# Attention into sorted rows: per-side waits for the copies of batch 7, and fewer comparisons of counts

## The chip, the cores and the metric

The kernel runs on 1 core of a Trainium2 chip. The metric is the device time of one execution in microseconds (us). Three runs of the kernel before gave 193.85, 194.16 and 194.34 us; the median is 194.16 us.

## What is computed

The first half is an attention without a softmax over pairs: with 8 batches, 8 heads, 576 tokens and 64 channels per head, q is normalised by its exponentials over the channels, k by its exponentials over the tokens, kv = kᵀv per head, and the result is q·kv. The second half is a mixture of experts on the 4608 tokens with 512 channels:

```python
x = attn_out.transpose(0, 2, 1, 3).reshape(N, D)          # N = 4608, D = 512
logits = x @ w_gate + modality_bias[modality_id]
e_idx = argmax(logits, 1)
out[mask] = gate_w[mask, None] * (relu(x[mask] @ w1[e]) @ w2[e])   # for each expert e
```

The kernel takes it that each of the two modalities ends at the expert that its bias prefers. It therefore runs two experts only, counts at the end whether that was true, and has a loop over all experts for the case that it was not (it runs zero times on this data).

## The kernel before, in words

**Sorted rows.** The tile xs (128 partitions x 4 x 4608 columns, bf16) holds the attention's output transposed, one column per token, sorted by modality: side a fills from column 0 upwards, side b from column 4607 downwards. A batch has 9 groups of 64 tokens. Inside a group a permutation (line 1128) has brought the tokens of side a to the front. After the multiplication with kv (line 1167) the group lies in PSUM, and the function put (line 1183 and on) copies its 64 columns twice into xs (line 1198): once for side a at the number of a-tokens so far, once for side b. The place is a register value. Each copy writes all 64 columns, and what does not belong to its side is overwritten by a later copy of the same side. The very last group is written by both sides at the same place.

**What makes the copies wait.** As the place is not known ahead, the function window gives the framework a stand-in range of columns, and the framework makes a copy wait for earlier instructions that wrote or read the same stand-in range. In batches 0 to 6 the two sides have ranges of their own. In batch 7 both sides have the same one, the 64 columns around the middle column MID = 2304, so that each copy waits for the end of the copy before it, whichever side that was.

**Who copies.** A planner (class Plan, with a table of due times, TUNED) orders all work by a model of costs before anything is issued; its order is the order of each engine's queue. In batches 6 and 7 all 18 copies are on ScalarE (ACT). In batch 6 they alternate a, b, a, b. In batch 7 the order is b0 a0 b1 a1 b2, a ReLU (line 1274), then b3 a2 b4 a3 b5 a4 a5, then a load of two register values (line 1444) and a copy of a quarter of the expert weights (line 1467), then b6 a6 b7 a7 a8 b8.

**What reads the rows.** The function ffn runs a pass over 256 columns of one side: logits (line 1240), then the first matrix in four steps of 8 matmuls, function h_mm (line 1312), ReLU on VectorE (line 1276) or ScalarE (line 1274), the second matrix (line 1325), the scaling by the gate (line 1282) and an indirect DMA of the rows to DRAM (line 1285). Passes 0 to 6 of a side follow their batches. The four passes of batch 7 (two of each side, around MID) and one more for the tile in which the two sides meet wait for every copy of batch 7. PSUM has a ring of buffers; a buffer that a copy still reads can't be written by the next matmul.

**Around it on VectorE.** At the same time VectorE runs mid_run (lines 827 to 838), twelve small instructions that sort out the rows of the tile in the middle, the ReLUs and the evictions of line 1142. The code behind the plan (lines 1594 to 1644) checks counts: 16 comparisons of the running number of a-tokens (in aoff_x, one row) with limits (lines 1630 and 1633), a matmul that sums the tokens with the expected expert (line 1621), a minimum over all results (line 1641), and the number of times that the fallback loop runs. The framework places these instructions on its own, and the trace shows 15 of the comparisons between and right behind the instructions of mid_run.

Of the kernel before, what the change touches and what calls it, by code (L numbers as in the profile page):

```python
# [10 lines left out]
FP32 = mybir.dt.float32  # L11
# [4 lines left out]
ALU = mybir.AluOpType  # L16
# [3 lines left out]
P = 128  # L20
# [10 lines left out]
def view(t, dims, off=0, parts=None):  # L31
    p0 = t.ap[0]
    if parts is None:
        return bass.AP(tensor=t.tensor, offset=t.offset + off, ap=[list(p0)] + [list(d) for d in dims])
    lo, n = parts
    return bass.AP(
        tensor=t.tensor, offset=t.offset + lo * p0[0] + off, ap=[[p0[0], n]] + [list(d) for d in dims]
    )
# [206 lines left out]
def kernel(  # L245
# [12 lines left out]
    nc = tc.nc  # L258
    B, H, S, Dh = q.shape
    D = H * Dh  # L260
    N = B * S
# [3 lines left out]
    NJ = S // 64  # L265
    NC = B * NJ
# [4 lines left out]
    MID = N // 2  # L271
    TM = MID // P
    GW = 256
    RW = P

    passes_a = [(n, 256 * n, 256) for n in range(B)] + [(B - 1, 256 * B, 256)]
# [8 lines left out]
    def sb(shape, dtype, name):  # L285
        return pool.tile(shape, dtype, name=name)
# [43 lines left out]
    place = sb([P, NSL], FP32, "place")  # L330
# [316 lines left out]
    aoff_x = sb([1, NC + 1], FP32, "aoff_x")  # L647
# [9 lines left out]
    both = sb([P, 2, 2], FP32, "both")  # L657
# [203 lines left out]
    o_bsel = pl.op({"POOL": (2.3, 2.4, True)}, bsel_run, [o_aoff, o_exp], key="bsel", rank=13)  # L861
    o_mid = pl.op({"DVE": (1.0, 1.15, True)}, mid_run, [o_idx, o_bsel], key="mid", rank=74)

    def window(at, of_pass, T):

        n, lo, w = of_pass
        off = lo + (w - T) // 2 if n < B - 1 else MID - T // 2
        return bass.AP(
            tensor=xs.tensor,
            offset=xs.offset + at,  # L870
            ap=[list(xs.ap[0]), [N, KD], [1, T]],
            dep_tracking_offset=xs.offset + off,
        )

    final, edge, scaled_q = [], {}, []

    def sync(later, first, reason):
        tc.add_manual_dep(
            later.ins,
            first.ins.name,  # L880
            mybir.DependencyInfo(mybir.DependencyClass.Sync, mybir.DependencyReason.DATA),
            reason=reason,
        )
# [8 lines left out]
    def attention(b):  # L892
# [227 lines left out]
        for gi, (j0, nj) in enumerate(groups):  # L1120
            sbuf = Buf(r_ps)
            w = nj * 64
# [39 lines left out]
        for gi, (j0, nj) in enumerate(groups):  # L1162
            xbuf = Buf(r_ps)

            def s2(_, j0=j0, nj=nj, xbuf=xbuf):
                for c in range(KD):
                    nc.tensor.matmul(  # L1167
                        out=view(ps_t[xbuf.idx], [[1, nj * 64]], c * nj * 64),
                        lhsT=kvbd[kvb.idx][:, c, :],
                        rhs=et[etb.idx][:, c, j0 * 64 : (j0 + nj) * 64],  # L1170
                        start=True,
                        stop=True,
                    )

            o3 = pl.op(
                on_pe(*[nj * 64] * KD),
                s2,
                [ets[gi], o_kb],
                key=own_key(f"s2_{b}", j0), rank=R + 4,
                takes=[xbuf],  # L1180
                uses=[kvb, etb],
                lag=lag,
            )
            for jj in range(nj):
                for side in range(2):

                    def put(e, jj=jj, j0=j0, nj=nj, side=side, xbuf=xbuf):
                        c = b * NJ + j0 + jj
                        a = av[e][(j0 + jj) // 2]
                        if j0 + jj < NJ - 1:  # L1190
                            a = a >> 16 if jj else a & 0xFFFF
                        a = nc.s_assert_within(a, 0, 64 * c, skip_runtime_bounds_check_because=WHY)
                        if side:
                            a = a + (N - 64 - 64 * c)
                        p = next(x for x in (passes_b if side else passes_a) if x[0] >= b)
                        dst = window(a, p, 64)
                        src = view(ps_t[xbuf.idx], [[nj * 64, KD], [1, 64]], jj * 64)
                        w_ = nc.scalar.copy(out=dst, in_=src) if e == "ACT" else nc.vector.tensor_copy(out=dst, in_=src)  # L1198
                        if b >= 3 and not started["ab"[side]]:
                            started["ab"[side]] = True  # L1200
                            for before in id_ins:
                                sync(w_, before, "windows overlap the digits of places")
                        if not j0 + jj and b:
                            sync(w_, edge[side], "windows of the batch before reach into this one's")
                        if j0 + jj == NJ - 1:
                            edge[side] = w_
                        if b == B - 1:
                            final.append(w_)

                    before = win[-2] if len(win) > 1 else filled[b - 1][side - 2] if b else None  # L1210

                    across = win[-1 - 2 * side] if j0 + jj == NJ - 1 and b == B - 1 else None
                    same = before and before.costs.keys() == {copier[b][side]}
                    win.append(
                        pl.op(
                            on_dve(256) if copier[b][side] == "DVE" else on_act(256),
                            put,
                            [o3, o_id if b >= 3 else None, *los, None if same else before, across],
                            key=own_key(f"put{b}{side}", j0 + jj), rank=R + 4, gap=0.13,
                            uses=[xbuf],  # L1220
                        )
                    )
                    if same:
                        pl.follow(win[-1], before)
            if copier[b][0] != copier[b][1]:

                for o in win[-2 * nj + 1 :: 2]:
                    pl.later(o, win[-2])
# [8 lines left out]
    def logits(t0, nt, t, whole=False):  # L1237
        for i in range(nt):
            for c in range(KD):
                m = nc.tensor.matmul(  # L1240
                    out=t[:, i * E : (i + 1) * E],
                    lhsT=xs[:, c, (t0 + i) * P : (t0 + i + 1) * P],
                    rhs=wg_sb[:, c, :],
                    start=(c == 0),
                    stop=(c == KD - 1),
                )
                if whole and not i and not c:
                    for w_ in final[-2:]:
                        sync(m, w_, "every batch is in its places")

    def gates1(t0, nt, t):
# [50 lines left out]
    def h_mm(t, lo, w, slot_, f0, whole=False, kds=(0, KD)):  # L1302

        if kds == (0, KD // 2):

            nc.tensor.matmul(
                out=t[:, 0 : 2 * w], lhsT=zero, rhs=view(ones, [[0, 2 * w // P], [1, P]], 0, (0, 1)), start=True, stop=False
            )
        for i in range(2):
            for kd in range(*kds):  # L1310
                f = f0 + i
                m = nc.tensor.matmul(  # L1312
                    out=t[:, i * w : (i + 1) * w],
                    lhsT=w1(W[:, slot_, :], kd, f),
                    rhs=xs[:, kd, lo : lo + w],
                    start=(kd == 0 and kds == (0, KD)),
                    stop=(kd == KD - 1 and (i == 1 or kds == (0, KD))),
                )
                if whole and not f and not kd:
                    for w_ in final[-2:]:  # L1320
                        sync(m, w_, "every batch is in its places")

    def y_mm(t, h, i, slot_, c0=0, cn=D, kfs=(0, KF)):
# [283 lines left out]
    def keys():  # L1607
# [11 lines left out]
    nc.vector.tensor_copy(out=cnt_b, in_=cnt)  # L1619
    n_ps = ps_t[0]  # L1620
    nc.tensor.matmul(out=n_ps[:, 0:1], lhsT=ones, rhs=cnt_b, start=True, stop=True)
    early = sorted({(n, lo + w) for n, lo, w in passes_a if n < B - 1}) + [(B - 1, MID - RW)]
    ok = sb([1, 1 + 2 * len(early)], FP32, "ok")
    nc.vector.tensor_scalar(
        out=ok[:, 0:1], in0=n_ps[0:1, 0:1], scalar1=float(N) - 0.5, scalar2=None, op0=ALU.is_ge
    )
    for i, (n, need) in enumerate(early):
        so_far = aoff_x[0:1, NJ * (n + 1) : NJ * (n + 1) + 1]
        o_ = 1 + 2 * i
        nc.vector.tensor_scalar(  # L1630
            out=ok[:, o_ : o_ + 1], in0=so_far, scalar1=float(need), scalar2=None, op0=ALU.is_ge
        )
        nc.vector.tensor_scalar(
            out=ok[:, o_ + 1 : o_ + 2],
            in0=so_far,
            scalar1=float(S * (n + 1) - need),
            scalar2=None,
            op0=ALU.is_le,
        )
    okm = sb([1, 1], FP32, "okm")  # L1640
    nc.vector.tensor_reduce(out=okm, in_=ok, op=ALU.min, axis=AX.X)
# [2 lines left out]
        out=nrest, in0=okm, scalar1=-float(E), scalar2=float(E), op0=ALU.mult, op1=ALU.add  # L1644
# [11 lines left out]
    with tc.For_i(0, nr) as e:  # L1656
# [21 lines left out]
        for part in range(2):  # L1678
            nc.sync.dma_start(
                out=view(st[2 + part], [[D, 4], [1, D]]),  # L1680
# [70 lines left out]
```

## Time and profile before

| | |
|---|---|
| time of the profiled execution | 193.99 us |
| its span, first to last instruction | 192.4 us |
| granted TensorE clock, mean | 0.991 of full speed |
| TensorE matmul busy | 178.2 us (93% of the span) |
| VectorE busy | 144.3 us (75%) |
| ScalarE busy | 127.5 us (66%) |
| GpSimd busy | 101.9 us (53%) |
| chain that ended last | PE 63%, DVE 12%, issue 8%, ACT 7%, DMA 6% |

PE is TensorE's matmul queue, PEld its weight loads, DVE VectorE, ACT ScalarE, POOL GpSimd. Starts are in us from the first instruction of the profiled execution. Matmuls are pipelined: one starts while the one before is still running, and the ends are modelled.

### The profile page before, as it was taken

Reading aid. Unit: us, or ns where it says so; the run is one execution under the profiler, and the core shown is the slowest. Engines: PE = TensorE matmul, PEld = TensorE weight load, DVE = VectorE, ACT = ScalarE, POOL = GpSimd, SP = SyncE. Lnnn points to the kernel's source line nnn. Section 1 sums busy time; section 2 is a strip of 40 time slices with the busy share of each in tenths; the row PEclk is TensorE's granted clock in tenths of the full one; section 3 lists DMA queues with packets and bytes.
Section 4 is the critical chain, followed back from the end, with each engine's and each line's share of the span. In section 5 each row is a group of like instructions: output and inputs, shape, how many; then the busy total and the mean of one; then the engine's idle time right before and its main releaser. Section 6 shows DMA issues by size and latency. Waiting matters only on the chain.

```text
span 192.4 us, 4978 instructions
## 1 busy us (share of the span) xinstructions
PE 178.2 (93%) x1743; PEld 124.2 (65%) x1759; DVE 144.3 (75%) x393; ACT 127.5 (66%) x251; POOL 101.9 (53%) x130
## 2 busy tenths in 40 slices
PE   1899999999999999999999999999998999999970
PEld 0545458586884687579658866884883975664740
DVE  4898979999989377659789899796596674364750
ACT  2756988887749099999898896699598980100000
POOL 7058987285917729846548753745812203504441
PEclk9999999999999999999999999999999999999996
DMA  5999999999999999999997773100300301412202
GB/s 202 388 396 393 224 203 211 256 391 314 191 401 353 413 407 411 332 393 411 335 336 247 237 291 114 58 2 0 148 20 0 114 0 55 167 55 109 98 28 101
DMA packets 18077, 42.34 MB, mean 220 GB/s; under 512 B 1393, under 2 KB 1393, under 8 KB 18050
## 3 DMA queue, kind: packets, MB, share of 16 engines
q1 hardware_dynamic: 12816, 28.31, 40.8%
q0 software_dynamic: 5200, 13.64, 24.6%
q8 instruction: 14, 0.23, 0.5%
q14 instruction: 13, 0.11, 0.2%
q10 hardware_dynamic: 34, 0.05, 0.1%
HBM read 36.75 MB, written 9.70 MB: 241 GB/s over the span
## 4 chain that ended last, share of the span: by engine, by line
PE 63%; DVE 12%; issue 8%; ACT 7%; DMA 6%; POOL 1%; ACTq 0%; DVEq 0%; POOLq 0%
PE ps L1325 24%; PE ps L1312 24%; DMA st<-in_k_dram 4%; PE ps L1044 4%; PE ps L1167 3%; PE ps L1128 3%; DVE own L914 3%; DVE xs L1198 2%; PE ps L1240 2%; DMA st<-in_q_dram 2%; ACT st L908 1%; ACT xs L1198 1%; DVE xs L767 1%; DVE y_sb L1282 1%; ACT y_sb L1280 1%
## 5 line engine op out<-in xcount | busy, mean ns | idle before, releaser
L1312 PE MATMUL ps<-xs,W 128*128 128x256 bf16 x576 | 68.6, 273 | 0.6 <-ACT y_sb L1280 0.3
L1325 PE MATMUL ps<-W,hT 128*128 128x512 bf16 (+1 forms) x281 | 64.8, 373 | 0.9
L1285 POOL DMA_INDIRECT out_dram<-y_sb,idx x36 | 35.5, 986 | 54.0 <-DVE y_sb L1282 40.7
L1312 PEld LDWEIGHTS <-W 128*128 128x128 bf16 x576 | 54.5, 98 | 8.6 <-issue 2.2
L1325 PEld LDWEIGHTS <-hT 128*128 128x128 bf16 x296 | 28.1, 98 | 29.1 <-issue 0.2
L930 POOL TENSOR_TENSOR eq<-st,qi 128x512 bf16<-128x512 f32 (+1 forms) x38 | 36.0, 974 | 11.6 <-PE ps L1167 4.5
L1282 DVE TENSOR_SCALAR y_sb<-ps,gate 128x512 f32<-128x512 f32 (+1 forms) x30 | 22.0, 732 | 19.1 <-PE ps L1325 13.3
L1198 ACT CAST xs<-ps 128x256 f32 (+1 forms) x90 | 29.9, 428 | 2.9 <-PE ps L1167 1.0
L1276 DVE TENSOR_SCALAR hT<-ps 128x512 bf16<-128x512 f32 x35 | 23.7, 684 | 5.5 <-PE ps L1312 3.9
L914 DVE TENSOR_REDUCE own<-st 128x18 f32<-128x1152 f32 x16 | 21.7, 1356 | 4.2 <-ACT st L908 4.2
L1274 ACT ACTIVATE hT<-ps 128x512 bf16<-128x512 f32 x37 | 21.3, 603 | 2.9 <-PE ps L1312 2.1
L908 ACT ACTIVATE st<-st 128x1152 f32<-128x1152 f32 x16 | 18.5, 1178 | 6.5 <-issue 4.4
L941 ACT ACTIVATE ek<-st 128x1152 bf16<-128x1152 f32 x16 | 18.9, 1180 | 3.1 <-DMA st<-in_k_dram 3.1
L1198 DVE CAST xs<-ps 128x256 f32 (+1 forms) x54 | 19.9, 418 | 0.6 <-issue 0.2
L1140 ACT CAST et<-ps 128x512 bf16<-128x512 f32 (+1 forms) x30 | 15.8, 556 | 5.4 <-PE ps L1128 4.2
L951 POOL CAST vb<-st 128x1152 bf16<-128x1152 f32 x8 | 9.1, 1149 | 9.6 <-DMA st<-in_v_dram 9.6
L1593 PE MATMUL ps<-ones 128*128 128x512 bf16 x39 | 12.8, 454 | 1.2 <-POOL ones L340 1.2
L1128 PE MATMUL ps<-perm,eq 128*128 128x128 bf16 x144 | 12.7, 222 | 0.4 <-POOL eq L930 0.2
L1167 PE MATMUL ps<-et,kvbd 128*128 128x128 bf16 (+1 forms) x160 | 11.8, 214 | 0.2
L1128 PEld LDWEIGHTS <-eq 128*128 128x128 bf16 x144 | 9.9, 99 | 3.1 <-DVE eq L930 1.0
L1167 PEld LDWEIGHTS <-kvbd 128*128 128x128 bf16 x160 | 10.0, 98 | 2.6 <-issue 0.6
L1044 PE MATMUL ps<-vb,ek 64*128 64x129 bf16 x288 | 10.8, 223 | 0.9 <-issue 0.4
(142 smaller groups left out, 168.3 us busy)
## 6 DMA issues: line engine op xcount, KB each, us to landing
st<-in_k_dram SPq DMA_DIRECT2D x5, 1152.0 KB, 12.3
st<-in_v_dram SPq DMA_DIRECT2D x5, 1152.0 KB
st<-in_q_dram SPq DMA_DIRECT2D x5, 1152.0 KB, 9.2
st<-in_q_dram SPq DMA_DIRECT2D x6, 576.0 KB, 5.2
st<-in_k_dram SPq DMA_DIRECT2D x6, 576.0 KB, 8.8
st<-in_v_dram SPq DMA_DIRECT2D x6, 576.0 KB, 10.2
W<-in_moe_w_dram POOLq DMA_DIRECT2D x8, 256.0 KB
W<-in_moe_w_dram POOLq DMA_DIRECT2D x4, 512.0 KB
```

The source lines that it names most:

```text
L908: nc.scalar.activation(out=t, in_=t, func=ACT.Exp)
L914: nc.vector.tensor_reduce(out=sums[qib.idx][:, h * NJ : (h + n) * NJ], in_=view(st[bq.idx], [[Dh, n * NJ], [1, Dh]], h * NJ * Dh), op=ALU.add,
L930: (nc.vector if e == "DVE" else nc.gpsimd).tensor_tensor(out=view(eq[eqb.idx], [[HG * Dh, n], [Dh, HG], [1, Dh]], j0 * HG * Dh), in0=view( ...
L1128: nc.tensor.matmul(out=view(t, [[2 * nj * 64, 2], [1, 64]], hp * nj * 64 + jj * 64), lhsT=eq[eqb.idx][:, j0 + jj, P * hp : P * hp + P], rh ...
L1167: nc.tensor.matmul(out=view(ps_t[xbuf.idx], [[1, nj * 64]], c * nj * 64), lhsT=kvbd[kvb.idx][:, c, :], rhs=et[etb.idx][:, c, j0 * 64 : (j0 ...
L1198: w_ = nc.scalar.copy(out=dst, in_=src) if e == "ACT" else nc.vector.tensor_copy(out=dst, in_=src)
L1274: nc.scalar.activation(out=dst, in_=src, func=ACT.Relu)
L1276: nc.vector.tensor_scalar_max(out=dst, in0=src, scalar1=0.0)
L1282: nc.vector.tensor_scalar(out=dst, in0=src, scalar1=g, scalar2=None, op0=ALU.mult)
L1285: s_ = nc.gpsimd.indirect_dma_start(out=out, out_offset=bass.IndirectOffsetOnAxis(ap=ix[:, c : c + 1], axis=0), in_=ysb, in_offset=None, b ...
L1312: m = nc.tensor.matmul(out=t[:, i * w : (i + 1) * w], lhsT=w1(W[:, slot_, :], kd, f), rhs=xs[:, kd, lo : lo + w], start=(kd == 0 and kds = ...
L1325: nc.tensor.matmul(out=t, lhsT=h[:, kf, i * P : (i + 1) * P], rhs=W[:, slot_, W2 + kf * D + c0 : W2 + kf * D + c0 + cn], start=(kf == 0), ...
```

## The change

The stand-in range of batch 7 becomes one for each side, 64 columns below MID for side a and 64 columns above for side b. The copies of the last group of batch 7 get explicit waits for the last copies that both sides have issued so far. The readers of the last passes get explicit waits for both last copies, in every one of the four steps of h_mm (before: in the first step only). The 16 one-element comparisons become two comparisons over 7 counts each and two of one element; the limits 256, 512, ... come from a row of the tile place, and the upper limits are 1.25 times the lower ones.

```diff
-    def window(at, of_pass, T):
+    def window(at, of_pass, T, side):
         n, lo, w = of_pass
-        off = lo + (w - T) // 2 if n < B - 1 else MID - T // 2
+        off = lo + (w - T) // 2 if n < B - 1 else MID - T + T * side
...
                         if b == B - 1:
-                            final.append(w_)
+                            if j0 + jj == NJ - 1:
+                                for w in last_put.values():
+                                    sync(w_, w, "both sides meet in the last window")
+                                final.append(w_)
+                            last_put[side] = w_
...
                 if whole and not i and not c:          # logits
-                    for w_ in final[-2:]:
+                    for w_ in final:
...
-                if whole and not f and not kd:         # h_mm
-                    for w_ in final[-2:]:
+                if whole and not i and not kd:
+                    for w_ in final:
                         sync(m, w_, "every batch is in its places")
...
-    for i, (n, need) in enumerate(early):
-        so_far = aoff_x[0:1, NJ * (n + 1) : NJ * (n + 1) + 1]
-        o_ = 1 + 2 * i
-        nc.vector.tensor_scalar(out=ok[:, o_ : o_ + 1], in0=so_far, scalar1=float(need), ..., op0=ALU.is_ge)
-        nc.vector.tensor_scalar(out=ok[:, o_ + 1 : o_ + 2], in0=so_far, scalar1=float(S * (n + 1) - need), ..., op0=ALU.is_le)
+    need = view(place, [[2, B - 1]], 2, (0, 1))
+    so_far = view(aoff_x, [[NJ, B - 1]], NJ)
+    nc.vector.tensor_tensor(out=ok[:, 1:B], in0=so_far, in1=need, op=ALU.is_ge)
+    nc.vector.scalar_tensor_tensor(
+        out=ok[:, B : 2 * B - 1], in0=need, scalar=(S - 2 * P) / (2 * P), in1=so_far, op0=ALU.mult, op1=ALU.is_ge
+    )
+    for i, (limit, op) in enumerate(((MID - RW, ALU.is_ge), (N - (MID - RW), ALU.is_le))):
+        nc.vector.tensor_scalar(out=ok[:, 2 * B - 1 + i : 2 * B + i], in0=aoff_x[0:1, NC : NC + 1], scalar1=float(limit), ..., op0=op)
```

## Rows read from the trace of the kernel before

**Rows 1.** Chain that ended last, 136 to 152 us: start, length, what.

```profile
140.39 0.38 ACT xs L1198
...
140.82 2.85 PE ps L1312 x24
...
148.37 0.76 DVE y_sb L1282
```

**Rows 2.** Busy time of the engines by stretch; columns PE, PEld, DVE, ACT, POOL, clock, DMA.

```profile
144.50:149.10 4.60, 3.78 (x19) 1.66 (x17) 2.94 (x5) 4.07 (x8) 1.01 (x1) 1.00 0.00 0
149.10:158.00 8.90, 8.83 (x100) 7.31 (x102) 5.79 (x29) 8.52 (x15) 0.98 (x1) 1.00 0.16 62
158.00:187.00 29.00, 28.44 (x197) 17.99 (x197) 15.90 (x23) 1.76 (x3) 10.69 (x11) 1.00 0.22 83
```

**Rows 3.** Waits of PE and PEld, 130 to 192 us: total, times, longest.

```profile
PE ps L1240 <- DVE y_sb L1282: 0.8, 1, 0.8
...
PEld L1240 <- ACT xs L1198: 1.3, 1, 1.3
```

**Rows 4.** Timeline of PE and PEld: start, length, what, idle before it.

```profile
140.22 0.50 PE L1128 MATMUL ps<-perm,eq 128*128 128x128 bf16 x6
...
140.82 2.85 PE L1312 MATMUL ps<-xs,W 128*128 128x256 bf16 x24
140.82 2.56 PEld L1312 LDWEIGHTS <-W 128*128 128x128 bf16 x23 [0.22 <-issue]
...
144.72 3.62 PE L1325 MATMUL ps<-W,hT 128*128 128x512 bf16 x15
...
149.12 0.95 PE L1240 MATMUL ps<-wg_sb,xs 128*128 128x8 bf16 x32 [0.79 <-DVE y_sb L1282]
...
149.93 6.27 PE L1312 MATMUL ps<-xs,W 128*128 128x256 bf16 x56
```

**Rows 5.** Timeline of ACT in batch 7.

```profile
139.18 1.99 ACT L1198 CAST xs<-ps 128x256 f32 x5 [1.04 <-PE ps L1167]
141.07 0.60 ACT L1274 ACTIVATE hT<-ps 128x512 bf16<-128x512 f32 x1
141.55 2.81 ACT L1198 CAST xs<-ps 128x256 f32 x7
144.87 1.90 ACT L1467 COPY st<-W 128x2048 bf16 x1 [0.51 <-DVE hT L1276]
146.68 2.39 ACT L1198 CAST xs<-ps 128x256 f32 x6
```

**Rows 6.** Line 1198 in batch 6, then twice in batch 7: ns min/median/max, first and last start.

```profile
L1198 ACT CAST xs<-ps x16: 412/514/537, 129.7 to 133.8; 128x256 f32 x16
...
L1198 ACT CAST xs<-ps x5: 372/373/375, 139.2 to 140.8; 128x256 f32 x5
...
L1198 ACT CAST xs<-ps x6: 366/372/374, 146.7 to 148.7; 128x256 f32 x6
```

**Rows 7.** Line 1444, the load of register values on ACT.

```profile
L1444 ACTq TENSOR_LOAD <-over_i x1: 504/504/504, 144.0 to 144.0; - x1
```

**Rows 8.** Timeline of DVE in batch 7.

```profile
140.27 0.14 DVE L1630 TENSOR_SCALAR ok<-aoff_x 1x1 f32<-1x1 f32 x1
140.34 0.13 DVE L1633 TENSOR_SCALAR ok<-aoff_x 1x1 f32<-1x1 f32 x1
...
141.41 0.22 DVE L838 SCALAR_TENSOR_TENSOR idx_x<-both,over 128x1 int32<-128x1 f32 x1
141.54 0.13 DVE L1633 TENSOR_SCALAR ok<-aoff_x 1x1 f32<-1x1 f32 x1
...
141.91 0.67 DVE L1276 TENSOR_SCALAR hT<-ps 128x512 bf16<-128x512 f32 x1
142.51 1.00 DVE L1142 CAST et<-ps 128x512 bf16<-128x512 f32 x2
```

**Rows 9.** The page's costliest groups: line 1312 (busy, mean ns of one, idle before).

```profile
L1312 PE MATMUL ps<-xs,W 128*128 128x256 bf16 x576 | 68.6, 273 | 0.6 <-ACT y_sb L1280 0.3
```

**Rows 10.** Timeline from 187 us: the last DMA issue.

```profile
187.39 0.97 POOL L1285 DMA_INDIRECT out_dram<-y_sb,idx  x1 [0.51 <-DVE okm L1641]
```

More of the change, by code (lines that the diff above doesn't have):

```diff
@@ L873, in window @@
         )
-    final, edge, scaled_q = [], {}, []
+    final, edge, last_put, scaled_q = [], {}, {}, []
     def sync(later, first, reason):
@@ L1195, in put @@
                         p = next(x for x in (passes_b if side else passes_a) if x[0] >= b)
-                        dst = window(a, p, 64)
+                        dst = window(a, p, 64, side)
                         src = view(ps_t[xbuf.idx], [[nj * 64, KD], [1, 64]], jj * 64)
@@ L1621 @@
     nc.tensor.matmul(out=n_ps[:, 0:1], lhsT=ones, rhs=cnt_b, start=True, stop=True)
-    early = sorted({(n, lo + w) for n, lo, w in passes_a if n < B - 1}) + [(B - 1, MID - RW)]
-    ok = sb([1, 1 + 2 * len(early)], FP32, "ok")
+    ends_a = sorted({(n, lo + w) for n, lo, w in passes_a if n < B - 1})
+    assert ends_a == [(n, 2 * P * (n + 1)) for n in range(B - 1)]
+    ok = sb([1, 1 + 2 * B], FP32, "ok")
     nc.vector.tensor_scalar(
@@ L1626 @@
     )
-    for i, (n, need) in enumerate(early):
-        so_far = aoff_x[0:1, NJ * (n + 1) : NJ * (n + 1) + 1]
-        o_ = 1 + 2 * i
-        nc.vector.tensor_scalar(
[L1631 to L1638, printed above, removed]
+    need = view(place, [[2, B - 1]], 2, (0, 1))
[5 more added lines that the diff above has]
+    for i, (limit, op) in enumerate(((MID - RW, ALU.is_ge), (N - (MID - RW), ALU.is_le))):
+        nc.vector.tensor_scalar(
+            out=ok[:, 2 * B - 1 + i : 2 * B + i], in0=aoff_x[0:1, NC : NC + 1], scalar1=float(limit), scalar2=None, op0=op
         )
```

## The prediction

> **What bounds the kernel now.** I read the chain of waits first. In the stretch of batch 7 the work that ended last runs through the copies of line 1198 on ScalarE into 24 matmuls, and later through an eviction on VectorE into the logits of the last passes [rows 1]. Then the busy time by stretch: from 149.1 us TensorE is busy for 8.83 of 8.90 us and 28.44 of 29.00, at a granted clock of 1.00, so from there the end follows TensorE; in the stretch before, 144.5 to 149.1, it is busy for only 3.78 of 4.60 us [rows 2]. The list of waits names that hole: the logits' first matmul waited 0.79 us, their first weight load 1.3 us, and the two name different engines, which is a question for later [rows 3]. So time is to be had only where TensorE stood still before 149.12.
>
> I measure these holes by the spacing of matmuls, since one starts while the last still runs. In the run of 56 matmuls of line 1312, (6.27 - 0.27) / 55 = 0.109 us lie between starts, with 0.27 for the last one's own length [rows 4, 9].
> - Hole 1: before the 24 matmuls at 140.82 the weight loader was idle for 0.22 us [rows 4].
> - Hole 2: those 24 took 2.85 us, (2.85 - 0.27) / 23 = 0.112 each, so 23 x 0.003 = 0.07 us is lost between the groups of eight [rows 4].
> - Hole 3: line 1325 shows 15 matmuls (one of 16 has no record) from 144.72 in 3.62 us, which is 0.216 each with 0.38 for the last; the next could have started at 144.72 + 16 x 0.216 = 148.17 and did at 149.12: 0.95 us [rows 4].
>
> Together 1.24 us, the most that the change can give here.
>
> **The change, part 1: waits of the copies.** Before, a copy of batch 7 starts when the last one has ended: (148.7 - 146.7) / 5 = 0.40 us apart, of which 0.37 is its own length [rows 6]. Batch 6 shows the new pattern on the same engine, since there each copy waits only for its own side: 16 copies in alternation start (133.8 - 129.7) / 15 = 0.27 us apart, though each takes 0.51 [rows 6]. So I take 0.13 us off wherever the two sides alternate. It stays at 0.40 (or goes up to 0.51 + 0.03, if the first of the two is lengthened as in batch 6) where a copy follows its own side or is the last group: a5 behind a4, a8 behind b7 and a7, b8 behind a8.
>
> In order of time, with the first copy at 139.18 as before (it waits for TensorE, [rows 5]):
> 1. The fourth copy starts at 139.18 + 3 x 0.27 = 139.99, not 140.39, and ends by 140.50, not 140.77. The 24 matmuls start 0.05 after that copy's end now [rows 1, 4], so by 140.55. Hole 1 goes.
> 2. The fifth copy follows at 140.26, the ReLU of line 1274 at 140.53, and 0.49 behind it, as now [rows 5], the next copy at 141.02. Five more at 0.27 bring a4 to 142.37, and a5 comes at 142.8 to 142.9, where it was 144.0. The load of registers (0.50, [rows 7]) and the copy of weights follow: the latter started 0.88 after a5, so it is at 143.7 to 143.8, not 144.87.
> 3. That copy holds ScalarE 1.81 us up to the next one [rows 5]: b6 at 145.5 to 145.6, then a6, b7, a7 at 0.27, then a8 and b8 at 0.40 to 0.54. The last starts at 147.1 to 147.5 and ends at 147.5 to 147.9, where it ended at 149.06.
> 4. TensorE, ahead by the 0.29 of holes 1 and 2, is ready for the logits at 148.17 - 0.29 = 147.88. Hole 3 is gone, or nearly (0.05 if the slow end holds).
>
> What is late next is TensorE itself. The copies of weights behind the last put move with it on the same queue, 1.1 us earlier or more, and the DMAs are issued by POOL on evictions that follow TensorE; the last of them is issued at 187.39 and all that is behind it moves along [rows 10].
>
> The added waits in 12 more groups of h_mm are satisfied when they are reached. I cost them at nothing, because the 56 matmuls of [rows 4] are seven groups that wait each for a buffer, without a gap at 0.109. From the other side, a wait could let the array run empty: 0.273 - 0.109 = 0.16 us each [rows 9].
>
> **Part 2: comparisons.** The 16 comparisons sit at 140.27 to 144.1 on VectorE. Each takes 0.13 us, but the next starts 0.06 to 0.07 later [rows 8]. Most fill pauses in the chain of mid_run; behind its last instruction at 141.41 stand six in a row, from 141.54 to 141.91, and they hold up the ReLU of line 1276 by 0.37 us [rows 8]. The third group of the 24 matmuls begins when that ReLU has ended (141.91 + 0.67 = 142.58), so without part 2 TensorE would get there early and wait: hole 1 would come back as a hole here. With the six gone the ReLU starts at 141.55 and ends at 142.22; TensorE, 0.29 ahead, asks for it at 142.3. The four new ones are not in the trace. One over 7 elements on one partition I take at 0.06 to 0.07 of the queue like its neighbours; the bounds are nothing (all in pauses) and 4 x 0.14 = 0.56 (none pipelined, all in front of the ReLU). At 0.07 in pauses they cost nothing. All four behind mid_run would leave 0.09 of the 0.37, and some 0.2 of the gain here would go; the upper bound would put the ReLU 0.19 later than now and take all of the 0.29 and 0.19 more, which leaves 1.24 - 0.48 = 0.76 us, 193.4. The evictions of line 1142 that follow (142.51, [rows 8]) move with the ReLU. At the end of the program nothing changes: the minimum still runs over 17 results.
>
> **Sum.** 0.22 + 0.07 + 0.95 = 1.24 us off the profiled execution's 193.99 (span 192.4 and 1.6 around it): 192.75. The median of the three runs is 0.17 above that execution, so 192.9 us.
>
> A rule that speaks against part 1: the Trainium skill, "VectorE: DVE Perf Modes", section "The DRAIN you can't avoid", says of VectorE that the next operation doesn't start until the pipe is empty, that a semaphore between two operations costs nothing extra, and that one should minimise the count of operations, not of semaphores. Carried over to ScalarE, part 1 would give nothing, and only part 2 would count. The trace disagrees: on ScalarE copies of 0.51 start 0.27 apart, and on VectorE comparisons of 0.13 start 0.06 apart [rows 6, 8].
>
> **Rivals.**
> - *The eviction, not the copy, releases the logits.* The matmul's row names y_sb of line 1282, which ran from 148.37 to 149.13 right behind TensorE's own line 1325 [rows 1, 3]. Then hole 3 follows TensorE and stays; only holes 1 and 2 go: 194.16 - 0.29 = 193.9. For it: the row and the chain. Against: the weight load, which comes first, names the copy, and the logits read nothing that the eviction writes. 10%.
> - *A part stays.* The four comparisons stand in front of the ReLU, or the copies come at 0.30 and not 0.27, so that a5, a8 and b8 leave some 0.3 us of hole 3: 0.4 to 0.5 less gain, 193.3 to 193.4. For it: b8's end has only 0.0 to 0.35 to spare. 16%.
> - *The copies stay 0.40 apart*, because the pipe empties between them or the framework still orders the sides by something else. Then holes 1 and 3 stay and only hole 2's wait for the ReLU shrinks: 194.16 - 0.04 = 194.1. Against: batch 6. 7%.
> - *Slower: the new waits break TensorE's stream.* 12 groups x 0.16 = 1.9 us: 192.9 + 1.9 = 194.8. It outweighs the gain from 1.24 / 12 = 0.10 a wait. For it: they are at the stage that sets the end. Against: groups with satisfied waits run without a gap [rows 4]. 5%.
>
> **How the numbers follow.** The forecast has 62%, with its own range 192.6 to 193.2 (the runs differ by 0.5, and 0.05 of hole 3 may stay). What a measurement here can tell from no change is about 0.3%, 0.58 us: faster means below 193.6, slower above 194.7. Forecast and nearly all of "a part stays" are faster: 0.76. The eviction, the unchanged copies and the rest are the same: 0.19. Slower 0.05. The range runs from 192.5 (all of the holes, and a low draw of the runs) to 193.9: it leaves out the unchanged copies and the slower case, 12%, the upper half of the draws of the eviction's case, 5%, and a few per cent below 192.5.
>
> **What would show it.** In the profile after: copies of batch 7 that start 0.27 apart in alternation and 0.4 to 0.5 apart at a5, a8, b8; the 24 matmuls at about 140.55 with a spacing of 0.109; the ReLU of line 1276 at about 141.55; the copy of weights at about 143.7; the logits at about 147.9 with no wait on ScalarE; everything after 149.1 us moved by the same 1.2 us. Wrong would be: logits that still start 0.9 us behind line 1325, or a first gain that is given back in front of the ReLU or between 149 and 187 us.

## The result, and the profile after

The median is 192.65 us (192.31 to 193.46, 7 runs) against 194.34 us (193.85 to 195.36, 7 runs) of the kernel before on the same chip: a ratio of 0.9909, 95% interval [0.988, 0.9939]. The ratios here and below use the fast runs alone and are not the quotients of the medians, from which they differ by up to 0.2%. The profiled execution took 193.11 us, its span is 191.5 us. The lines behind 1198 that are named below have numbers four higher than before (1240 is 1244, 1276 is 1280, 1312 is 1316, 1325 is 1329); the copies are still line 1198.

The chain that ended last, 136 to 152 us after the change (start, length, what; its last pieces), answers to [rows 1]:

```profile
140.76 0.34 PE ps L1128 x6
141.10 2.62 PE ps L1316 x24
...
145.20 3.19 PE ps L1329 x14
148.39 0.78 PE ps L1244 x32
```

No copy and no eviction stands in it any more: TensorE follows on TensorE, also in the pieces left out, but for 0.05 us. The busy time by stretch (PE, PEld, DVE, ACT, POOL, clock, DMA), against [rows 2]; the first stretch begins 0.4 us and ends 0.9 us earlier than there, the others lie 0.9 us earlier:

```profile
144.10:148.22 4.12, 4.07 (x23) 2.16 (x23) 2.58 (x5) 4.05 (x8) 0.43 (x1) 1.00 0.00 0
148.22:157.10 8.88, 8.83 (x101) 7.29 (x101) 6.04 (x29) 8.25 (x15) 1.55 (x2) 1.00 0.17 62
157.10:186.10 29.00, 28.43 (x197) 18.00 (x197) 15.90 (x23) 1.76 (x3) 10.66 (x11) 1.00 0.22 83
```

In the first stretch TensorE was busy for 3.78 of 4.60 us and is now for 4.07 of 4.12, so it stands idle for 0.05 us and not 0.82; the two behind it are as they were. The timeline of TensorE in batch 7 (start, length, what, idle before it), against [rows 4]:

```profile
140.60 0.50 PE L1128 MATMUL ps<-perm,eq 128*128 128x128 bf16 x6
140.94 2.78 PE L1316 MATMUL ps<-xs,W 128*128 128x256 bf16 x24
...
144.77 3.62 PE L1329 MATMUL ps<-W,hT 128*128 128x512 bf16 x15
148.22 0.95 PE L1244 MATMUL ps<-wg_sb,xs 128*128 128x8 bf16 x32
149.03 6.27 PE L1316 MATMUL ps<-xs,W 128*128 128x256 bf16 x56
```

The 24 matmuls take 2.78 and not 2.85 us, the logits have no idle time before them, and the 56 matmuls take 6.27 us as before. The timeline of ACT, against [rows 5]:

```profile
139.57 1.48 ACT L1198 CAST xs<-ps 128x256 f32 x5 [1.05 <-PE ps L1167]
140.89 0.65 ACT L1278 ACTIVATE hT<-ps 128x512 bf16<-128x512 f32 x1
141.38 2.22 ACT L1198 CAST xs<-ps 128x256 f32 x7
144.10 1.90 ACT L1471 COPY st<-W 128x2048 bf16 x1 [0.50 <-DVE et L1142]
145.91 2.00 ACT L1198 CAST xs<-ps 128x256 f32 x6
```

Five copies in 1.48 and not 1.99 us, seven in 2.22 and not 2.81, six in 2.00 and not 2.39. By line 1198 alone (ns min/median/max, first and last start), against [rows 6], each copy takes longer by the profile and they start closer together:

```profile
L1198 ACT CAST xs<-ps x7: 373/467/502, 141.4 to 143.2; 128x256 f32 x7
```

And DVE, against [rows 8]; the six comparisons in front of the ReLU are gone, and the four new ones stand in pauses:

```profile
140.67 0.16 DVE L1634 TENSOR_TENSOR ok<-aoff_x,place 1x7 f32<-1x7 f32 x1
140.82 0.15 DVE L1635 SCALAR_TENSOR_TENSOR ok<-place,aoff_x 1x7 f32<-1x7 f32 x1
140.89 0.13 DVE L1639 TENSOR_SCALAR ok<-aoff_x 1x1 f32<-1x1 f32 x1
...
141.16 0.13 DVE L1639 TENSOR_SCALAR ok<-aoff_x 1x1 f32<-1x1 f32 x1
...
141.78 0.22 DVE L838 SCALAR_TENSOR_TENSOR idx_x<-both,over 128x1 int32<-128x1 f32 x1
141.92 0.69 DVE L1280 TENSOR_SCALAR hT<-ps 128x512 bf16<-128x512 f32 x1
...
148.43 0.75 DVE L1286 TENSOR_SCALAR y_sb<-ps,gate 128x512 f32<-128x512 f32 x1 [0.92 <-PE ps L1329]
```

**One number for each kernel.** The profiled executions start batch 7 at slightly different times (139.18 us before, 139.57 after), from stages that the change doesn't touch. So I compare *the stretch*: the time from the start of batch 7's first copy to the start of the first logits matmul, by the starts of the single instructions. Before it is 149.12 - 139.18 = 9.94 us, after 148.22 - 139.57 = 8.66 (the rows are rounded): 1.28 us less. From the logits to the last instruction it is 43.29 us before and 43.30 after, and 43.27 to 43.41 in all kernels below, so what the stretch loses the program loses.

### The profile page after: what moved, and what is told of

It reads as the page before. It is cut to its first block, busy times and chain, and to the rows that moved or that the text cites. A ratio compares the mean times of both kernels' runs of the same rounds, so it can differ in the third digit from the quotient of the medians.

```text
span 191.5 us, 4965 instructions
## 1 busy us (share of the span) xinstructions
PE 178.2 (93%) x1743; PEld 124.6 (65%) x1759; DVE 143.6 (75%) x381; ACT 126.6 (66%) x251; POOL 101.7 (53%) x130
## 4 chain that ended last, share of the span: by engine, by line
PE 85%; ACT 4%; DVE 3%; DMA 2%; issue 2%; POOL 1%; ACTq 0%
PE ps L1316 33%; PE ps L1329 32%; PE ps L1044 5%; PE ps L1128 4%; PE ps L1167 3%; DMA st<-in_q_dram 2%; PE ps L1244 2%; PE ps L1597 2%; DVE own L914 1%; ACT st L908 1%; ACT xs L1198 1%; PE ps L1482 1%; ACT et L1140 1%; PE ps L1513 1%; PE ps L808 1%
## 5 line engine op out<-in xcount | busy, mean ns | idle before, releaser
L1198 ACT CAST xs<-ps 128x256 f32 (+1 forms) x90 | 28.8, 435 | 2.6 <-PE ps L1167 1.0
L1044 PEld LDWEIGHTS <-ek 64*128 64x128 bf16 x288 | 9.0, 99 | 3.5 <-issue 3.0
```

## Experiments

Theory: the copies stood late against TensorE, TensorE waited for them in the three holes of the prediction, and the change is worth these holes; part 1 (the waits of the copies) fills them, part 2 (the comparisons) only keeps a fourth from opening. Rivals: part 2 alone does it, by fewer operations on VectorE; the removed order between the copies doesn't matter, only where the last ones stand; or the holes belong to something else.

The kernels ran on three chips: chip A (the first four), chip B (six) and chip C (the last two). Ratios are to the kernel before on the same chip, whose medians were 192.07 us on A, 193.77 (beside the first two kernels there) and 194.03 (beside the other four) on B, 192.18 on C.

**Chip A: the parts of the change.** The changed kernel once more, unedited:

> The changed kernel once more, as the measure for the others in the same session. I read two things: the time against the kernel before, and in the trace the stretch from the first copy of batch 7 (line 1198) to the first matmul of the logits behind it (line 1244): 9.94 us before (139.18 to 149.12), 8.65 in the changed kernel's first profile (139.57 to 148.22). Theory: 8.65 again and a ratio near 0.993 (1.29 us of 194). Rival (the first ratio of 0.991 is the true one, and 0.4 us came from elsewhere): the stretch again 8.65, but the ratio again 0.991 or less.

The change without part 2, that is, with the 16 comparisons of before:

```diff
-    need = view(place, [[2, B - 1]], 2, (0, 1))
-    so_far = view(aoff_x, [[NJ, B - 1]], NJ)
-    nc.vector.tensor_tensor(out=ok[:, 1:B], in0=so_far, in1=need, op=ALU.is_ge)
...
+    for i, (n, need) in enumerate(early):
+        so_far = aoff_x[0:1, NJ * (n + 1) : NJ * (n + 1) + 1]
...
```

> Part 1 alone: copies wait for their own side, the 16 comparisons stay. Theory: copies 0.27 us apart and the hole before the 24 matmuls gone, but the ReLU of line 1280 still stands behind six comparisons, some 2.73 us behind the first copy, and the third group of eight matmuls waits for it, so the 0.29 us of the first holes come back there: the stretch is 9.94 - 0.95 = 8.99 us, ratio near 0.995. Rival (the comparisons only fill pauses of VectorE and part 2 is worth nothing): 8.65 us, with no gap in front of the third group, and a ratio equal to that of the whole change.

The change without part 1:

```diff
-        off = lo + (w - T) // 2 if n < B - 1 else MID - T + T * side
+        off = lo + (w - T) // 2 if n < B - 1 else MID - T // 2
...
```

> Part 2 alone: 4 comparisons, but both sides of batch 7 share one stand-in range as before. Theory: copies stay 0.40 us apart, hole 1 (0.22 us) and hole 3 (0.95 us) stay, only the 0.04 us in front of the third group goes: the stretch is 9.90 us, ratio 1.000. Rival (the ReLU is what TensorE waits for in this stretch, and its 0.37 us count in full): 9.57 us, ratio 0.998.

The change with explicit waits that put the first 12 copies of batch 7 in a chain again:

```diff
+                        if b == B - 1 and j0 + jj < 6:
+                            for w in chain[-1:]:
+                                sync(w_, w, "one after the other")
+                            chain.append(w_)
```

> The changed kernel, with an explicit wait of each of the first 12 copies of batch 7 for the copy before it; the last six, right in front of the logits, stay free. Theory: ScalarE's queue carries the delay. The copy of weights starts 5.70 us behind the first copy as it did before (4.54 in the changed kernel), the last six start 1.2 us later than in the changed kernel, their last ends at 9.50, and the stretch is 9.55 us: of the 1.29 us only 0.4 stay, ratio near 0.998. Rival (the six copies that the logits directly wait for carry the gain; the first 12 have a copy of weights and slack behind them): 8.65 to 8.9 us, ratio near that of the whole change.

The copies were spaced as meant in all four, but TensorE was not ready for the logits until 9.56 us after the first copy. The three kernels with the new waits all came out there, where the changed kernel had shown 8.66, so these runs don't separate them. The first two missed their numbers by that (8.65 and 8.99 us were expected), and the chain of twelve met its 9.55 us for another reason than the expected one:

| kernel, chip A | stretch | median | ratio |
|---|---|---|---|
| changed, again | 9.56 | 191.73 | 0.9995 [0.9972, 1.0017] |
| waits only | 9.56 | 191.61 | 0.9976 [0.9964, 0.9989] |
| comparisons only | 9.95 | 192.08 | 1.0008 [0.9993, 1.0023] |
| chain of the first 12 | 9.56 | 191.75 | 0.9977 [0.9959, 0.9995] |

What differs is where the first copy stands. Timelines on chip A, the changed kernel, of ACT and then of TensorE:

```profile
137.39 1.48 ACT L1198 CAST xs<-ps 128x256 f32 x5
...
146.95 0.95 PE L1244 MATMUL ps<-wg_sb,xs 128*128 128x8 bf16 x32
```

The profile shows no idle time ahead of the copy, where the kernels before and after had 1.04 us and 1.05 us in the first runs. The ReLU on VectorE shows the same: in the changed kernel's first run, and then on chip A:

```profile
139.45 0.69 DVE L1280 TENSOR_SCALAR hT<-ps 128x512 bf16<-128x512 f32 x1 [1.08 <-PE ps L1167]
```

```profile
137.12 0.69 DVE L1280 TENSOR_SCALAR hT<-ps 128x512 bf16<-128x512 f32 x1
```

So on chip A the copies are 9.56 - 8.66 = 0.90 us earlier against TensorE's own stream. With the old waits only one hole is left there, before the logits (TensorE, comparisons only):

```profile
139.58 2.78 PE L1312 MATMUL ps<-xs,W 128*128 128x256 bf16 x24
...
147.26 0.96 PE L1240 MATMUL ps<-wg_sb,xs 128*128 128x8 bf16 x32 [0.23 <-ACT xs L1198]
```

By the starts it is 9.95 - 9.56 = 0.39 us, 0.2% (the row counts only from the modelled end of the matmul ahead): all that the change can give on this chip, and too little for the ratio of the changed kernel to show. The ratios of the two other kernels with the new waits, 0.9976 and 0.9977, agree with it. Part 2 alone gives nothing: the stretch of the kernel before was 9.94 us in its first profile (it was not profiled again on this chip). The chain of twelve costs nothing, since the copies still end 0.07 us ahead of the logits.

**Chip B: the chain.** All 18 copies in a chain, then only the last six:

```diff
-                        if b == B - 1 and j0 + jj < 6:
+                        if b == B - 1:
```

```diff
-                        if b == B - 1 and j0 + jj < 6:
+                        if b == B - 1 and j0 + jj >= 6:
```

> The changed kernel with an explicit wait of every copy of batch 7 for the one before it, so that the stand-in ranges are the new ones and the waits the old ones. Theory (the wait alone is what the ranges change): copies 0.40 us apart, the two holes of 0.22 and 0.95 us are back, the stretch is 9.90 us as with the comparisons alone, ratio 1.000. Rival (the new ranges matter in another way too, by what they make the readers in the last passes wait for): the stretch is 9.5 us or less although the copies are 0.40 apart.

> The changed kernel, with an explicit wait of each of the last six copies of batch 7 for the one before it; the first 12 stay free. Theory: the copy of weights stays 4.54 us behind the first copy and the first of the six at 6.34; five spacings of 0.40 put the last one's end at 8.74, 0.05 later the logits: the stretch is 8.79 us, only 0.14 longer than the 8.65 of the changed kernel, ratio near 0.994. Rival (these six carry the gain): the 0.39 us that they lose (3 x 0.13) show in full, 9.04 us or more, ratio 0.995 or more.

Here the first copy was late again. ACT with all 18 in a chain, then TensorE:

```profile
139.38 2.00 ACT L1198 CAST xs<-ps 128x256 f32 x5 [1.09 <-PE ps L1167]
...
149.32 0.96 PE L1248 MATMUL ps<-wg_sb,xs 128*128 128x8 bf16 x32 [0.82 <-DVE y_sb L1290]
```

With that chain the stretch is 9.94 us, the time 194.05, the ratio 0.9998 [0.9967, 1.0029]: everything of the change but the freed order of the copies is worth nothing together, part 2 included. With the last six alone in a chain it is 8.79 us, as the theory had it, 193.0 us, 0.9945 [0.9912, 0.9979]; those six carry 0.13 of the 1.28 us. ACT there, then TensorE:

```profile
139.64 1.48 ACT L1198 CAST xs<-ps 128x256 f32 x5 [1.04 <-PE ps L1167]
...
145.99 2.39 ACT L1198 CAST xs<-ps 128x256 f32 x6
...
148.43 0.95 PE L1248 MATMUL ps<-wg_sb,xs 128*128 128x8 bf16 x32
```

**Chip B: the two that chip A couldn't answer.** The same kernels with the waits only, and with the chain of the first 12:

> The waits alone (new windows, 16 comparisons) once more. The theory of the prediction: where ScalarE's first copy and VectorE's ReLU start about 1 us behind the matmul that they wait for, the later ReLU holds the third group of eight matmuls by 0.3 us: a gap there, the logits at about 8.99 us after the first copy against 8.66 in the changed kernel, and the time 0.3 us above that of the changed kernel. Where they start right behind that matmul, 9.56 us and no gap, as the first run had. The rival (the ReLU has slack in either case): no gap, 8.65 us or 9.56 us.

> The changed kernel with a chain through the first 12 copies once more. The theory: where the first copy starts about 1 us behind its matmul, the first twelve copies are 0.40 apart again, the logits come at 9.5 to 9.6 us after the first copy and nearly all of the gain is gone (0.9 of the 1.29 us); where it starts right behind, 9.56 us and no gap, as the first run had. The rival (the last six carry the gain): 8.65 to 8.9 us where the first copy is late.

The waits only: 9.01 us (8.99 expected), 193.33 us, ratio 0.9968 [0.9949, 0.9987]. The gap before the third group of eight is there, and it names the ReLU (the row has 0.18 us from the modelled end of the matmul ahead; by the starts, 16 at 0.109 us, it is 142.64 - 140.56 - 1.74 = 0.34). ACT and TensorE, then DVE:

```profile
139.18 1.48 ACT L1198 CAST xs<-ps 128x256 f32 x5 [1.04 <-PE ps L1167]
...
140.56 1.91 PE L1316 MATMUL ps<-xs,W 128*128 128x256 bf16 x16
142.64 1.03 PE L1316 MATMUL ps<-xs,W 128*128 128x256 bf16 x8 [0.18 <-DVE hT L1280]
...
148.18 0.94 PE L1244 MATMUL ps<-wg_sb,xs 128*128 128x8 bf16 x32
```

```profile
141.42 0.22 DVE L838 SCALAR_TENSOR_TENSOR idx_x<-both,over 128x1 int32<-128x1 f32 x1
141.56 0.13 DVE L1637 TENSOR_SCALAR ok<-aoff_x 1x1 f32<-1x1 f32 x1
...
141.92 0.67 DVE L1280 TENSOR_SCALAR hT<-ps 128x512 bf16<-128x512 f32 x1
```

So part 2 is worth 9.01 - 8.66 = 0.35 us on top of part 1, and nothing without it. The chain of the first 12: 9.54 us, 193.77 us, 0.9983 [0.9962, 1.0004], with the copies of those twelve 0.40 us apart; TensorE waits before the 24 matmuls and for the last copy again:

```profile
139.67 1.99 ACT L1198 CAST xs<-ps 128x256 f32 x5 [1.05 <-PE ps L1167]
...
141.31 2.81 PE L1320 MATMUL ps<-xs,W 128*128 128x256 bf16 x24
...
149.21 0.95 PE L1248 MATMUL ps<-wg_sb,xs 128*128 128x8 bf16 x32 [0.42 <-ACT xs L1198]
```

The first twelve copies carry 0.88 of the 1.28 us. With the last six the sum is 1.01 and not 1.28: in the changed kernel the last copy ends at 8.34 us of the stretch, 0.27 us before it would hold up the logits (which start 0.05 us behind it where they wait). A chain of the last six moves that end by 0.40 us: alone it costs 0.40 - 0.27 = 0.13, and behind twelve late copies the full 0.40.

**Chip B: all copies later.** Is it the lateness of the copies that sets the gain? Two copies of 512 columns into a scratch tile delay the others, in the kernel before and in the changed one. They were meant to stand behind the second copy of batch 7; the traces show them behind the first:

```diff
+                        if b == B - 1 and not j0 + jj and side:
+                            for _ in range(2):
+                                nc.scalar.copy(out=view(xx, [[1, KD * P]]), in_=view(ones, [[0, KD], [1, P]]))
```

> The kernel before with two copies of 512 columns into scratch put behind the second copy of batch 7, so that every later copy of that batch starts some 1.1 us later (estimate, twice a 512-column copy of ScalarE). The theory (the change is worth as much as the copies stand late against TensorE's own stream): the last copy and the logits move by the whole of it, 9.94 + 1.1 = about 11.0 us from the first copy to the logits, and the kernel is slower than before by 1.1 us (0.6%), or by a little less where a hole before the logits was partly idle for another reason. The rival (the gain differs with TensorE's own stream, not with the lateness of the copies): TensorE has slack here, the logits move by under 0.4 us.

> The changed kernel with the same two copies at the same place. The theory: its copies end at 8.34 + 1.1 = about 9.4 us after the first, so where TensorE is ready at 9.56 us nothing shows and the time is that of the changed kernel within 0.1 us, and the difference to the late kernel before grows from 0.39 to about 1.4 us (0.7%); where TensorE is ready at 8.66 us the logits move by about 0.8 us, and the difference to the late kernel before is about 1.5 us. The rival: the difference to the late kernel before stays what it is without the two copies, 0.39 us (0.2%) or 1.29 us (0.7%).

ACT of the kernel before, then TensorE:

```profile
138.28 0.38 ACT L1198 CAST xs<-ps 128x256 f32 x1 [1.02 <-PE ps L1167]
138.55 1.27 ACT L1201 COPY xx<-ones 128x512 bf16<-128x512 bf16 x2
...
149.26 0.95 PE L1243 MATMUL ps<-wg_sb,xs 128*128 128x8 bf16 x32 [0.82 <-DVE y_sb L1285]
```

The kernel before moved by the whole delay, 1.04 us: 10.98 us, 194.87 us, 1.0058 [1.0035, 1.008]. The changed one missed its number: 9.70 us, not 9.4 to 9.5 (193.84 us, 0.9997 [0.997, 1.0023]), and the difference of the two, 1.28 us, is the rival's. ACT and TensorE of the changed kernel show what I had left out:

```profile
138.41 0.38 ACT L1198 CAST xs<-ps 128x256 f32 x1 [1.01 <-PE ps L1167]
...
140.82 2.78 PE L1319 MATMUL ps<-xs,W 128*128 128x256 bf16 x24 [0.85 <-ACT xs L1198]
...
148.10 0.95 PE L1247 MATMUL ps<-wg_sb,xs 128*128 128x8 bf16 x32
```

The 24 matmuls wait for the fourth copy, which stands behind the delay; TensorE was itself moved by it, 8.66 + 1.04 = 9.70, so the lateness of the copies against TensorE was not changed. The pair shows that TensorE follows the copies here, and doesn't tell the theories apart.

**Chip C: TensorE later.** The other way round: four matmuls of zeros ahead of the 24, overwritten by what follows, so that the copies come earlier against TensorE, again in both kernels:

```diff
+                if b == B - 1 and j0 + nj == NJ:
+                    for _ in range(4):
+                        nc.tensor.matmul(out=t[:, 0 : 4 * P], lhsT=zero, rhs=view(ones, [[0, 4], [1, P]], 0, (0, 1)), start=True, stop=True)
```

> The kernel before with four more matmuls of 512 columns (0.87 us by the 0.218 between starts of line 1325) on TensorE, ahead of the last two permutation matmuls of batch 7 and so ahead of the 24 matmuls; they write zeros that the next matmuls overwrite. No copy waits for them. The theory (the gain is the time by which the copies stand late against TensorE's own stream): where the first copy starts about 1 us late, TensorE stands still for 1.24 us here and takes the 0.87 us in for nothing: the logits stay at 9.94 us after the first copy, the hole before them shrinks to some 0.4 us, and the time is that of the kernel before within 0.1 us. Where the first copy starts on time, the hole is 0.39 us and the logits move to 10.43 (0.49 us slower, 0.25%). The rival (the holes come with the chip or with something behind the copies, whatever TensorE's lead): the logits and the time move by the whole 0.87 us (0.45%).

> The changed kernel with the same four matmuls. The theory: TensorE has no hole left in this stretch, so the logits come 0.87 us later: at 8.66 + 0.87 = 9.53 us after the first copy where that copy is late, at 10.43 where it is on time. The difference to the kernel before with the same matmuls shrinks from 1.29 to about 0.4 us where the copy is late, and from 0.39 us to nothing where it is on time. The rival: that difference stays 1.29 us or 0.39 us.

This chip is one where the first copy is on time. ACT and TensorE with the old waits, then with the new ones:

```profile
137.19 2.00 ACT L1201 CAST xs<-ps 128x256 f32 x5
...
139.12 0.39 PE L1131 MATMUL ps<-perm,eq 128*128 128x128 bf16 x4
139.44 1.03 PE L1128 MATMUL ps<-ones,zero 1*128 1x512 bf16 x4
...
140.53 2.78 PE L1315 MATMUL ps<-xs,W 128*128 128x256 bf16 x24
...
147.82 0.94 PE L1243 MATMUL ps<-wg_sb,xs 128*128 128x8 bf16 x32
```

```profile
137.72 1.48 ACT L1201 CAST xs<-ps 128x256 f32 x5
...
141.07 2.78 PE L1319 MATMUL ps<-xs,W 128*128 128x256 bf16 x24
...
148.36 0.94 PE L1247 MATMUL ps<-wg_sb,xs 128*128 128x8 bf16 x32
```

From the permutation matmuls to the 24 it is 140.53 - 139.12 = 1.41 us and not 140.94 - 140.60 = 0.34, so the four cost 1.07 and not 0.87, and the 10.43 us that was expected became 10.63. Both kernels have the same stretch, 10.63 us = 9.56 + 1.07: the gain of the change is gone. If the kernel before has the stretch of 9.94 to 9.95 us here too (without the four it was not profiled on this chip), its hole has taken in 0.39 of the 1.07 us. The medians are 192.68 and 192.85 us, the ratios 1.0013 [0.9985, 1.0041] and 1.0028 [0.9999, 1.0057]. The rival's remaining difference of 0.39 us is not there in the stretch; the intervals of the ratios are too wide to tell it from nothing. So what the change gives is the time by which the copies were late: 1.28 us where they are late, 0.39 where they are less so, nothing where TensorE comes later still.

## Why the prediction was right, step by step

- *The holes.* Predicted 1.24 us as the most, measured 1.28 on the stretch; holes 1 to 3 are all gone. The 0.04 us more is hole 1: the prediction took the idle time of the weight loader, 0.22 us, but from the permutation matmuls to the 24 it was 0.60 us and is 0.34, so the hole was 0.26. The medians differ by 1.69 us (by the interval of the ratio, 0.0061 to 0.0120 of 194.34, it is 1.19 to 2.33), which holds the 1.28; the two profiled executions differ by 0.88, since the later one reached batch 7 0.39 us later. So the step is right by the trace, and the median's extra 0.4 us belongs to no part of the change that I can show.
- *The copies.* From the first copy on, by the prediction and by the trace after: a5 at 3.6 to 3.7 us and 3.66, the copy of weights at 4.5 to 4.6 and 4.53, b6 at 6.3 to 6.4 and 6.34, the end of b8 at 8.3 to 8.7 and 8.34, the logits at 8.70 and 8.66. The spacing read from batch 6 [rows 6] carried over.
- *Part 2.* The ReLU was to start 2.37 us after the first copy and started at 2.35, in front of TensorE's need. That it gives next to nothing by itself (0.04 us in the prediction's third rival, none with the chain of 18: 9.94) and that without it the 0.29 us of holes 1 and 2 come back (measured 0.35) was the step that I was least sure of.
- *The added waits* cost nothing: 56 matmuls in 6.27 us as in [rows 4]. The slower rival falls.
- *The eviction as releaser* falls too: line 1286 starts at 148.43, after the logits' first matmul at 148.22. In the trace before it ended at 149.13 and the last copy at 149.06, so the row in [rows 3] named the later of the two.
- *The rule of the Trainium skill.* In the Trainium skill, "VectorE: DVE Perf Modes", section "The DRAIN you can't avoid", a semaphore between VectorE's operations costs nothing extra. That the number of operations is to be kept small, and not that of the semaphores, stands in "Rules for kernel authors" of the same page, not where the prediction puts it. Carried over to ScalarE, as the prediction did, this would give part 1 nothing. The new waits with the old comparisons took the stretch from 9.94 to 9.01 us, and the fewer comparisons with every copy in a chain left it at 9.94: the measurement decides against the carry-over. The first of the two sections also says that a next operation that is not held starts earlier. Carried over in the same way, this sentence agrees with the copies, 0.27 us apart and not 0.40 once they don't wait for each other, and the prediction should have weighed it along with the other.
- *What was right by luck of the chip.* I took the idle 1.04 us before the first copy in [rows 5] as a part of the kernel. It is not: on chips A and C it is absent. On chip A hole 3 is 0.39 us and holes 1 and 2 are closed already, and the same change is worth 0.2%, and "no difference" would have been the right forecast. The prediction gave this no case of its own.

Open is why the first copy is late on some chips. That it is a matter of the chip is inferred from six late traces on chip B, and four and two on time on A and C; no run changed it by itself. The traces narrow it down: what comes late is the update of TensorE's semaphore, the counter on which ScalarE and VectorE wait, and not these engines (numbers below).

## What to carry to other kernels

Where instructions on one engine write disjoint places whose addresses the framework doesn't know, give them separate stand-in ranges, add explicit waits where the places do meet, and look for a stage of the same trace that already has them: its spacing is the price. Before believing in a hole on the bounding engine, ask what places the other engine against it; here a release of 1 us that came and went with the chip made 0.39 us into 1.28. And a small stall on a third engine may be worth nothing until the first one is repaired, then a quarter of the gain.

## What the runs showed of the hardware

- A release from TensorE that comes about 1 us late, to ScalarE and VectorE at once, at a granted clock of 1.00 in that stretch and with TensorE's own stream unchanged; on other chips it is absent. In all eight late traces ScalarE stands idle for 1.01 to 1.09 us before the first copy. The semaphore updates of the two matmuls that release the ReLU and the first copy are recorded there 1.32 to 1.40 and 1.10 to 1.19 us after these matmuls start, and 0.29 and 0.23 us after it in the six other traces; in all 14 the two engines start 0.02 and 0.08 us behind their updates. Before the change the medians on the chips without it lie 1.6 to 2.3 us lower (192.07 and 192.18 against 193.77 to 194.34), more than the 0.9 us that the late copies move.
- Four matmuls of 512 columns with one row of weights added 1.07 us to TensorE's queue. The second to the fourth start 0.216 us apart, as those of line 1329 do with 128 rows; the other 0.2 us stands at their two borders, 0.15 us from the last permutation matmul to the first of them (permutation matmuls are 0.056 apart) and 0.31 from the last of them to the next permutation matmul. What it is there is not shown.
